# Gated linear attention and a bilinear FFN on one core: the values term of four chunks in 128x32 tiles, with tokens put in order when y is evicted

## The chip, the cores and the metric

The kernel runs on one core of a Trainium2 chip. The metric is device time in microseconds (us): three runs of the kernel before gave 193.74, 194.33 and 194.84, median 194.33.

## What is computed

```python
# q, k, v, alpha: [4, 8, 768, 48] float32 (batch, head, token, dim)
for t in range(S):
    state = alpha[:, :, t, :, None] * state + einsum('bhd,bhe->bhde', k[:, :, t], v[:, :, t])
    y[:, :, t] = einsum('bhd,bhde->bhe', q[:, :, t], state)
x = y.transpose(0, 2, 1, 3).reshape(3072, 384)
out = ((x @ w_a) * (x @ w_b)) @ w_out        # w_a, w_b [384, 1536], w_out [1536, 384]
```

Each head carries a 48x48 state that decays by alpha at every token. The outputs of the eight heads stand side by side as the 384 inputs of the FFN.

## The kernel before

**Chunks.** The work is cut into six chunks. Chunk c covers two batches (`ch.b0`) and 256 tokens (`ch.s`), so chunks 0 and 1 are the first third of the sequence, 2 and 3 the second, 4 and 5 the last. A chunk has two units u (one per batch); the 256 tokens of a unit lie on 128 partitions, two neighbouring tokens per partition: token 2p + r is on partition p with rank r (`load`, L549). Partitions 0 to 63 and 64 to 127 are the groups g = 0 and 1, of 128 tokens each. HC is 64, C is 128, D is 48, DP is 64.

**Steps of one chunk**, by the names that the order uses:
- `ld a/k/q/v`: loads. v is cast to bfloat16 by the DMA, so GpSimd issues it (POOL's queue); a, k and q come from POOL's or SyncE's (SP's) queue.
- `ln`, `ra`, `l2`, `l2s`, `R`, `AQ` (or `H`, `L`, `A2`), `E`, `lv`, `mq`, `mk`: logarithms and cumulative sums of alpha, their exponentials, and q and k scaled by them into QKp (L678). `dr`, `dl` write and read the decays through DRAM for bls.
- `C`/`Ce` (chunks 0 and 1: PE transposes, L736, and their copies, L744 and L742) or `T` (chunks 2 to 5: DMA transposes from SP's queue, L767) give kqT, queries and keys with the dims on the partitions.
- `v`: copies the loaded values into the padded tile vxs, heads 96 apart, zeros between (L785 on ScalarE, L787 on VectorE). Two vxs tiles alternate between chunks.
- `K`, `K2`, `k`: the states (L799, L812 on PE; L826 to L830 on VectorE).
- `D`: scores of queries against keys (L841), 16 matmuls in 64x64 tiles, each 128 columns (queries) wide; group g of the keys goes to PSUM partitions of half g, rank rk to a block of the columns.
- `M` (L846) or `Mc` with `Mm` (L850, L854): the scores leave PSUM times the causal mask, as bfloat16 m.
- `SB`, `SA` (`carried`): queries times the carried states, opening the sums of y in two PSUM banks; `Y` (`inner`, L865): values times m added to them. Y takes 48 matmuls: 12 pieces of 64 rows of y (the 384 rows of a unit's y don't fall on head borders, so a piece covers parts of one or two heads, and the padding zeros keep the other heads out), times two ranks, times two groups, in 64x64 tiles.
- `X` (`evac`, L900, L902): evicts y into xT. In xT and all that follows, the columns of a 128-token block stand by rank, then by partition, not in token order.
- `a`, `b` (`ff`, L919): the two FFN products of 128 rows of d_ff, 3 matmuls each, 512 columns for a whole chunk (`*`) or 256 for a unit. `as` (L925): a's copy on ScalarE. `pr` (`ff_prod`, L933): their product on VectorE, which puts the tokens in order by a strided write. `o`, `oc` (L941, L952), `ot`, `otc` (L956, L958), `st`, `stc` (L974, L977): the last FFN product, 6 matmuls per half, its eviction and store.

**The order.** Every instruction's place is written out in the string PROGRAM: `chunk: step; step; ...`, with the engine (V, S, P, Y for VectorE, ScalarE, GpSimd, SyncE) or PSUM bank as the last argument. Each engine works its own instructions off in that order and waits where its data or a buffer is missing. FFN work of a chunk stands between the attention steps of the next. Beside L919, L941 and the like, PE has no other work. PSUM has eight banks; D, AQ and y take two neighbouring ones each. The a, k, q and v tiles have two buffers, m has four, `as_` three, xT two.

Of the kernel before, what the change touches and what calls it, by code (L numbers as in the profile page):

```python
# [53 lines left out]
0: as 0 1; b 6 * 0; b 11 * 3; a 8 * 4; pr 6 *; pr 11 *
2: ld a * P
0: b 0 1 1; as 8 *; a 3 1 6
1: E 0 b; lv 0 k V
0: a 10 * 2; pr 0 1
1: mq 0 V; ld v 1 P
0: b 8 * 4  # L60
1: A2 1 7
0: as 10 *; b 10 * 2; pr 8 *
1: E 1 b
0: as 3 1; as 7 *; b 9 * 3; b 3 1 0; b 7 * 1; a 9 * 6
2: ld q * P
1: v 0 S; lv 1 q V; mk 0 V
0: pr 10 *
1: mq 1 V; C 0 1 4
0: as 9 *
1: C 0 0 2  # L70
0: o 0 0 5; pr 7 *
1: dk * 6
2: ld k * P
3: ld v * P
0: cz 1 v P; pr 9 *
1: Ce 0 0 S; E 1 i; de *; lv 1 k P; Ce 0 1 V; D 0 1 1; D 0 0 3
0: pr 3 1
1: Mc 0 0; K2 0 0 7 0
0: o 1 0 6
1: mk 1 V; M 0 1  # L80
0: o 3 0 4; o 1 1 -; ot 1 S; c3 P
3: ld a * P
0: cs 1 0 P; o 3 1 -
1: k 0 0 V; k 0 1 V; Mm 0 0 V; SB 0 1; C 1 0 3; C 1 1 7
0: ot 3 S; o 0 1 -
1: Ce 1 0 V
2: ln *
1: v 1 V; D 1 0 3; Ce 1 1 S; K2 1 1 6 0; Y 0; SA 0
0: ot 0 V
1: k 1 0 V; D 1 1 6  # L90
0: o 2 0 5
1: M 1 0
2: l2 0 V
1: X 0 S; a 3 0 1; Mc 1 1
2: l2s 0 P; l2s 1 P
1: a 2 0 3; a 4 0 4
2: R 0
1: k 1 1 V; as 4 0
2: ra 1
1: as 3 0; b 4 0 7  # L100
0: o 2 1 -
1: as 2 0
0: ot 2 S
1: pr 4 0
2: R 1; lv 1 q P
1: b 3 0 6; b 2 0 7; a 5 0 2; pr 3 0; b 5 0 3; as 5 0; b 1 0 5; a 1 0 1; pr 5 0; pr 2 0; a 7 0 2; as 1 0; pr 1 0
2: AQ 3
1: SB 1 6
2: lv 0 k P
1: a 10 0 5  # L110
2: lv 1 k V; ra 0; ld v * P
1: Mm 1 1 V
2: E 1 b
1: as 10 0; b 10 0 0; pr 10 0
2: mq 1 V; E 1 i
1: as 7 0; b 7 0 1
2: E 0 b; E 0 i
1: a 0 0 5
0: st 3 Y
2: dr  # L120
1: SA 1; Y 1
2: mk 1 V
1: pr 7 0; a 11 0 0; a 6 0 3; b 6 0 2; X 1 S; b 11 0 4; a 2 1 6; as 6 0; a 3 1 7; as 11 0; b 2 1 1; pr 6 0
2: lv 0 q V
1: b 4 1 0; as 2 1
2: T 1
1: pr 11 0
2: dl
0: st 0 Y
1: a 0 1 2; pr 2 1  # L130
2: mq 0 V
1: b 3 1 3; b 0 0 6; as 3 1; as 0 0; b 0 1 7; pr 3 1; a 8 0 1; a 9 0 5
0: st 1 Y
1: b 8 0 3; b 9 0 4; pr 0 0; as 0 1
2: mk 0 V
1: a 4 1 2
3: ln *
1: a 9 1 6; pr 0 1; as 8 0; b 9 1 1
3: ra 1
1: b 10 1 7; pr 8 0; a 10 1 3; as 4 1; as 9 0; as 9 1; a 6 1 6; b 6 1 2; b 11 1 5; pr 4 1; as 10 1; pr 9 0; a 11 1 4; pr 10 1; pr 9 1; as 6 1  # L140
2: v 1 S
1: a 8 1 3; b 8 1 1; a 7 1 6; pr 6 1
3: l2 0 V
1: as 11 1
2: T 0
1: as 8 1; a 5 1 4
3: ra 0
1: as 5 1; a 1 1 2
2: v 0 V
4: ld a * Y  # L150
1: pr 11 1; as 7 1; pr 8 1
2: K2 * * 0 7; D 1 1 3; D 1 0 5
1: as 1 1; b 5 1 2; o 2 0 1
2: k * 0 V
1: pr 5 1
3: v 0 S; v 1 S
1: b 1 1 2
2: Mc 1 0; M 1 1
3: l2s 0 P; l2s 1 P
1: b 7 1 0; o 2 1 -; pr 1 1; o 3 0 4  # L160
2: SB 0 5
1: pr 7 1
3: R 0
2: D 0 0 2
1: ot 2 V
2: Mm 1 0 V
1: o 3 1 -
2: Mc 0 0; SB 1 0; D 0 1 2
3: R 1
1: ot 3 S  # L170
2: SA 0
1: o 0 0 4
0: cs 0 0 P
2: Mc 0 1
4: ln *
3: ld q * Y; ld k * Y
2: k * 1 V
3: AQ 2
2: Y 1; SA 1; Mm 0 1 V; Mm 0 0 V; Y 0; X 0 S
3: E 0 b  # L180
4: l2 0 V
2: X 1 V
1: o 0 1 -
2: b 1 * 6; a 1 * 5
3: E 1 b
4: ld k * Y
3: E 1 i
1: ot 0 S
3: E 0 i
4: l2s 0 P  # L190
2: a 0 * 0; b 0 * 1; as 0 *; as 1 *
3: lv 0 k P; lv 0 q P
2: a 5 * 7
1: st 3 Y
2: a 7 * 4
4: l2s 1 P
2: a 2 * 5
3: lv 1 q V; mq 1 V; lv 1 k V
2: pr 1 *
3: dr  # L200
2: pr 0 *
3: mk 0 V
4: ld q * Y
0: st 2 Y
2: as 5 *; a 6 * 6; b 6 * 2; as 7 *
3: mq 0 V
2: b 9 * 4; b 7 * 0
1: st 2 Y
3: dl
4: R 0  # L210
2: b 5 * 7
1: o 1 0 3
2: a 9 * 1; pr 7 *; as 6 *
3: T 0
2: pr 6 *
4: ra 0
2: pr 5 *; a 11 * 6
3: mk 1 V
2: as 9 *; a 3 * 0
4: lv 0 k V; lv 0 q V; R 1  # L220
2: as 2 *
1: o 1 1 -
2: as 11 *; a 8 * 5; b 11 * 2; a 4 * 7; b 2 * 1
3: T 1
1: ot 1 V
2: pr 9 *; as 8 *; pr 11 *; pr 2 *; b 8 * 3; b 4 * 5; as 4 *
5: ld a * Y
3: K2 * * 4 6
2: pr 8 *; as 3 *; pr 4 *
3: k * 0 V; D 0 0 2; Mc 0 0  # L230
2: b 3 * 1
4: ra 1
2: pr 3 *; b 10 * 5; a 10 * 0
3: D 1 0 1; D 1 1 3
2: as 10 *
3: k * 1 V; Mc 1 1
2: o 0 0 7; o 2 0 0
3: M 1 0
5: ln *
2: pr 10 *  # L240
4: lv 1 q P
3: SB 1 3; D 0 1 1; Mc 0 1
4: lv 1 k P
5: ld q * Y
1: st 0 Y
3: SB 0 5
2: o 2 1 -
3: Mm 1 1 V; Mm 0 0 V; Mm 0 1 V
4: ld v * P
2: ot 2 S; o 0 1 -  # L250
4: AQ 0; E 0 b; E 0 i
3: SA 0; Y 0; SA 1
4: E 1 b
3: Y 1
5: l2s 1 V
4: mq 0 V; mk 0 V
3: X 0 S; X 1 S
2: o 3 0 2; o 3 1 -
4: T 0
3: a 5 * 3  # L260
4: E 1 i; v 0 S
3: a 9 * 0
2: ot 3 S
3: b 5 * 6; a 6 * 5; as 5 *
2: st 2 Y
3: as 9 *
5: ld k * P; l2s 0 P
3: as 6 *
5: ra 1
4: mq 1 V  # L270
2: ot 0 S
3: a 0 * 1
4: mk 1 V
3: a 1 * 2
4: D 0 0 3
5: l2 0 V
1: st 1 Y
4: dr
5: R 0
3: pr 5 *  # L280
4: v 1 S; M 0 0
3: b 1 * 7; as 1 *; a 3 * 5; b 9 * 6; pr 9 *; b 6 * 4; a 2 * 0; pr 6 *
4: T 1
5: lv 0 k P
3: b 0 * 6; as 0 *; as 2 *
4: dl
3: a 8 * 1
5: lv 1 q P
3: b 4 * 0; a 4 * 4; b 2 * 3; pr 1 *; pr 0 *; as 8 *; pr 2 *; as 4 *; pr 4 *; b 3 * 6; b 8 * 2
5: ld v * P; lv 1 k P  # L290
3: a 11 * 1
5: ra 0
3: as 3 *; pr 8 *; as 11 *; a 7 * 0
4: D 1 0 3; K * 0 5
5: lv 0 q P
3: pr 3 *; as 7 *
5: v 1 V
4: k * 0 V
5: R 1
4: D 1 1 6; D 0 1 1; Mc 1 0; Mc 1 1; M 0 1  # L300
2: o 1 0 0; o 1 1 -
3: a 10 * 7; b 11 * 3
4: SB 1 4
2: ot 1 S
3: as 10 *
4: Mm 1 0 V
3: pr 11 *
4: SB 0 1
# [96 lines left out]
def kernel(  # L405
# [11 lines left out]
    nc = tc.nc  # L417
# [681 lines left out]
```

## Time and profile before

| | before |
|---|---|
| runs, us | 193.74, 194.33, 194.84 (median 194.33) |
| profiled execution: span from first to last instruction, us | 192.0 |
| the median's distance to that span, us (what lies around it; the page lists no other time of its own for the execution) | 2.3 |
| PE busy, us | 186.8 |
| VectorE (DVE), ScalarE (ACT), GpSimd (POOL) busy, us | 133.1, 106.5, 56.9 |
| granted TensorE clock | 1.00 |
| DMA packets, MB | 62618, 29.40 |
| read from HBM, MB | 25.98 |

The page's rows of digits cut the span into 40 slices of 4.8 us; a 9 is 90% busy or more. PE rows say when a matmul was in flight; since matmuls overlap, the time that one adds is read from the distance between the starts of neighbours, or from a piece of the chain, not from its own duration. The chain of waits follows the work back from the last instruction, at each step to what released it. The list of waits gives for each engine what ended its idle time.

### The profile page before, as it was taken

What the parts mean: (1) busy time and instruction counts of PE and PEld (TensorE: products, weight loads), DVE (VectorE), ACT (ScalarE), POOL (GpSimd) and SP (SyncE); (2) the same over time, 40 slices, a digit from 0 to 9 for tenths busy, and PEclk for the clock granted to TensorE, in tenths of its full rate; (3) what the DMA queues carried; (4) which work ended last, traced back from release to release, by engine and by line L of the source; (5) the groups of instructions that cost most, each with busy time, mean ns of one, the idle gap of its engine ahead of it and who ended that gap; (6) DMA issues with size and microseconds to landing.
All of it is one profiled execution on the core that took longest, in us unless ns stands there. A gap on an engine that the chain in (4) does not pass through costs nothing.

```text
span 192.0 us, 6086 instructions
## 1 busy us (share of the span) xinstructions
PE 186.8 (97%) x2613; PEld 116.9 (61%) x2613; DVE 133.1 (69%) x223; ACT 106.5 (55%) x194; POOL 56.9 (30%) x75
## 2 busy tenths in 40 slices
PE   7999999999999999999999999999999999999992
PEld 3888875677778876645557444656465644545562
DVE  2387698994989888899897956887567446252510
ACT  4448885656779867753487756743572435314211
POOL 8999626752450500640074262000000000000000
PEclk9999999999999999999999999999999999999999
DMA  5999999999969999999999989017641200000422
GB/s 132 274 219 218 251 253 235 244 269 264 251 107 166 165 216 265 248 254 149 233 213 181 156 174 129 3 42 140 146 66 44 85 0 0 0 0 3 164 82 82
DMA packets 62618, 29.40 MB, mean 153 GB/s; under 512 B 53712, under 2 KB 60768, under 8 KB 62592
## 3 DMA queue, kind: packets, MB, share of 16 engines
q0 software_dynamic: 18432, 13.37, 39.6%
q1 hardware_dynamic: 44016, 15.55, 38.1%
q8 instruction: 20, 0.33, 0.7%
q10 hardware_dynamic: 144, 0.10, 0.2%
q14 instruction: 6, 0.05, 0.1%
HBM read 25.98 MB, written 4.74 MB: 160 GB/s over the span
## 4 chain that ended last, share of the span: by engine, by line
PE 91%; DMA 5%; SPq 1%; DVE 1%; issue 1%; ACT 0%; DVEq 0%
PE psum L919 47%; PE psum L941 24%; PE psum L865 7%; PE psum L841 3%; DMA kqT<-QKp 3%; DMA q_t<-in_q_dram 3%; PE psum L736 2%; PE psum L633 1%; PE psum L952 1%; SPq L549 1%; PE psum L799 1%; PE psum L812 1%; PE psum L700 1%; PE psum L591 1%; PE psum L592 1%
## 5 line engine op out<-in xcount | busy, mean ns | idle before, releaser
L919 PE MATMUL psum<-xT,wb_t 128*128 128x512 bf16 (+1 forms) x270 | 56.0, 337 | 0.0
L919 PE MATMUL psum<-xT,wa_t 128*128 128x512 bf16 (+1 forms) x270 | 56.0, 337 | 0.0
L941 PE MATMUL psum<-wo_t,prod 128*128 128x384 bf16 x276 | 49.4, 326 | 0.0
L919 PEld LDWEIGHTS <-wb_t 128*128 128x128 bf16 x270 | 25.9, 98 | 19.9 <-issue 0.5
L919 PEld LDWEIGHTS <-wa_t 128*128 128x128 bf16 x270 | 25.9, 98 | 19.7 <-issue 0.3
L941 PEld LDWEIGHTS <-prod 128*128 128x128 bf16 x276 | 25.9, 98 | 17.6
L956 ACT ACTIVATE ot<-psum 128x384 f32<-128x384 f32 (+1 forms) x16 | 7.7, 482 | 22.7 <-PE psum L941 21.6
L850 ACT ACTIVATE m<-psum 128x1024 bf16<-128x1024 f32 x14 | 14.1, 1023 | 4.6 <-PE psum L841 4.3
L613 POOL TENSOR_TENSOR l<-la 64x384 f32<-64x384 f32 x7 | 7.8, 1108 | 26.6 <-ACT la L556 19.0
L846 DVE TENSOR_TENSOR m<-psum,mask 128x1024 bf16<-128x1024 f32 x10 | 12.1, 1220 | 3.1 <-PE psum L841 3.1
L652 POOL TENSOR_TENSOR q_t<-q_t,ra 128x384 f32<-128x384 f32 x5 | 6.1, 1215 | 22.5 <-ACT ra L645 19.7
L556 ACT ACTIVATE la<-a_t 128x1536 f32<-128x1536 f32 (+2 forms) x9 | 9.5, 1055 | 2.3 <-DMA a_t<-in_alpha_dram 2.2
L678 DVE TENSOR_TENSOR QKp<-q_t,beta 128x768 bf16<-128x768 f32 x10 | 10.0, 995 | 1.0 <-ACT beta L667 1.0
L865 PE MATMUL psum<-m,vx 64*64 64x128 bf16 x576 | 10.5, 217 | 0.0
L900 ACT ACTIVATE xT<-psum 128x768 bf16<-128x768 f32 x9 | 7.2, 816 | 5.7 <-PE psum L865 5.5
L678 DVE TENSOR_TENSOR QKp<-k_t,invb 128x768 bf16<-128x768 f32 x10 | 9.7, 972 | 0.8 <-ACT invb L667 0.8
L854 DVE TENSOR_TENSOR m<-m,mask 128x1024 bf16<-128x1024 bf16 x14 | 9.3, 684 | 1.2 <-ACT m L850 1.2
L958 DVE COPY ot<-psum 128x384 f32<-128x384 f32 (+1 forms) x9 | 4.8, 532 | 7.6 <-PE psum L941 4.7
L865 PEld LDWEIGHTS <-vx 64*64 64x64 bf16 x576 | 9.0, 107 | 0.5 <-issue 0.3
L841 PE MATMUL psum<-kqT 64*64 64x128 bf16 x384 | 9.0, 219 | 0.4 <-DMA kqT<-QKp 0.3
L652 POOL TENSOR_TENSOR k_t<-k_t,a_t 128x384 f32<-128x384 f32 x6 | 7.4, 1228 | 6.1 <-issue 3.3
L549 POOL DMA_DIRECT2D v_t<-in_v_dram x8 | 8.5, 1058 | 0.1
(271 smaller groups left out, 287.9 us busy)
## 6 DMA issues: line engine op xcount, KB each, us to landing
out_dram<-ot SPq DMA_DIRECT2D x23, 192.0 KB, 3.8
q_t<-in_q_dram SPq DMA_DIRECT2D x3, 768.0 KB, 6.5
a_t<-in_alpha_dram POOLq DMA_DIRECT2D x2, 768.0 KB, 15.2
k_t<-in_k_dram POOLq DMA_DIRECT2D x2, 768.0 KB, 12.1
v_t<-in_v_dram POOLq DMA_DIRECT2D x4, 384.0 KB, 7.0
a_t<-in_alpha_dram SPq DMA_DIRECT2D x2, 768.0 KB
k_t<-in_k_dram SPq DMA_DIRECT2D x2, 768.0 KB
a_t<-in_alpha_dram POOLq DMA_DIRECT2D x3, 384.0 KB, 8.5
```

The lines of the kernel that those rows point to most:

```text
L549: eng.dma_start(out=t[:, us, hs].rearrange("p b h r d -> p (b h) (r d)"), in_=src[ch.b0 + us.start:ch.b0 + us.stop, hs, ch.s * 2 * C:(ch.s ...
L556: nc.scalar.activation(out=ch.la[:, us, hs].rearrange("p b h r d -> p (b h r d)"), in_=ch.a[:, us, hs].rearrange("p b h r d -> p (b h r d) ...
L613: eng.tensor_add(ch.l2[(1 - g) * HC:(2 - g) * HC, 1], x[:, :, 0, :], x[:, :, 1, :])
L652: eng.tensor_mul(x, x, by)
L678: eng.tensor_mul(QKp[ch.c % 2][:, u, j, :, hs, :D], src[:, u, hs].rearrange("p h r d -> p r h d"), f)
L841: nc.tensor.matmul(s2[g * HC:(g + 1) * HC, r, p, rk, :], lhsT=turned_part(ch, u, 1, rk, 2 * h + p, g, rs), rhs=queriesT(ch, u, 2 * h + p, ...
L846: nc.vector.tensor_mul(m.rearrange("p r a k s -> p (r a) (k s)"), ch.s2[u, h].rearrange("p r a k s -> p (r a) (k s)"), maskn(4))
L850: nc.scalar.activation(out=m.rearrange("p r a k s -> p (r a) (k s)"), in_=ch.s2[u, h].rearrange("p r a k s -> p (r a) (k s)"), func=AF.Copy)
L854: eng.tensor_mul(x, x, maskn(4))
L865: nc.tensor.matmul(y[c * DP:(c + 1) * DP, g, j // 2 * C:(j // 2 + 1) * C], lhsT=lhsT, rhs=rhs, start=(g, c) not in begun, stop=False, skip ...
L919: nc.tensor.matmul(p, lhsT=(wa_t, wb_t)[w][:, kk, f * 128:(f + 1) * 128], rhs=ch.xT[:, kk, us, :], start=(kk == 0), stop=(kk == KT - 1))
L941: nc.tensor.matmul(op, lhsT=ch.prod[:, f, at:at + C], rhs=wo_t[:, f, :], start=(f == 0), stop=(f == NFF - 1))
```

## The change

For chunks 2 to 5 (`NR = 2`), the values term is written in other tiles:
- Values come from DRAM a second time, by four new DMAs per chunk (`lw`), straight into a padded tile vps: one DMA for each group g and rank rk, 64 partitions and 16 runs of 48 values each. In vps the two ranks of a group lie on the two halves of the partitions, and heads are 64 apart. vps is a view of vxs' storage; its zeros are set once per tile (`cz i w`) after chunks 0 and 1 are through with it. `K` reads the loaded v tile itself, and `v` is gone for these chunks.
- `D` writes rank rk to PSUM half rk and group g to a block of the columns. The mask for this form is copied from the old one (`cm2`).
- `Y` (`inner_rows`) sums over 128 partitions (both ranks of a group) at once and gives 32 rows of y per matmul: 16 slices times two groups, 32 matmuls in 128x32 tiles, four neighbours in different column quarters. It needs y opened by `SB` or `SA` before.

For all chunks, `X` is split into two evictions per unit, one per group, and each writes the tokens in order (a step of two columns); xT is laid out by 128-token block. `pr` then writes straight.

The order is written anew from the first line to the last, with the same number of `a`, `b`, `o`, `D`, `K`, `C` and `T` steps. Two `Ce` and three `ot` move from ScalarE to VectorE, and one `otc` the other way.

```diff
+    VP = D + DP // 2
+    NR = 2
+    mask2 = cst.tile([C, 2, HC], BF16, name="mask2")
     vxs = [cst.tile([C, 2, 2, H, VS], BF16, name=f"vx{i}") for i in range(2)]
+    vps = [t.rearrange("p b r h e -> p (b r h e)")[:, :4 * H * VP].rearrange("p (g b h e) -> p g b h e", g=2, b=2, h=H) for t in vxs]
...
+    def load_rows(ch, g, rk, eng):
+        at = ch.s * 2 * C + g * C
+        eng.dma_start(out=vps[ch.c % 2][rk * HC:(rk + 1) * HC, g, :, :, :D].rearrange("p b h d -> p (b h) d"),
+                      in_=v[ch.b0:ch.b0 + 2, :, at:at + C, :].rearrange("b h (s r) d -> r s (b h) d", r=2)[rk])
...
+    def values(ch, gs, u, rk, hd):
+        return ch.v[gs, u, hd, rk, :] if ch.c >= NR else vxs[ch.c % 2][gs, u, rk, hd, :D]
...
     def scores(ch, u, h, tag):
...
+                        rk, g = (y, x) if ch.c >= NR else (x, y)
                         rs = slice(r * DP, (r + 1) * DP)
-                        nc.tensor.matmul(s2[g * HC:(g + 1) * HC, r, p, rk, :], lhsT=turned_part(ch, u, 1, rk, 2 * h + p, g, rs),
+                        half, part_ = (rk, g) if ch.c >= NR else (g, rk)
+                        nc.tensor.matmul(s2[half * HC:(half + 1) * HC, r, p, part_, :], lhsT=turned_part(ch, u, 1, rk, 2 * h + p, g, rs),
...
+    SLICES = [(h, 3 * (h // 2) + j) for h in range(H) for j in ((0, 1) if h % 2 == 0 else (1, 2))]
+    RANKS = [[x for x in SLICES if x[1] % 4 == c] for c in range(4)]
+
+    def inner_rows(ch, u):
+        y, begun = ch.y[u]
+        vp = vps[ch.c % 2].rearrange("p g b h e -> p g b (h e)")
+        W32 = DP // 2
+        for n in reversed(range(len(SLICES) // 4)):
+            for g in range(2):
+                for c in range(4):
+                    h, j = RANKS[c][n]
+                    at = h * VP + W32 * j - D * h
+                    assert (g, c // 2) in begun
+                    nc.tensor.matmul(y[c * W32:(c + 1) * W32, g, j // 4 * C:(j // 4 + 1) * C], lhsT=vp[:, g, u, at:at + W32],
+                                     rhs=ch.m[u, h // 4][:, h % 2, h // 2 % 2, g, :], start=False, stop=False, skip_group_check=True)
...
-            ch.xT = wk.tile([128, KT, B, C], BF16, name="xT")
...
+            ch.xT = wk.tile([128, B, KT, C], BF16, name="xT")
+        evict(ch.xT[:, 2 * u + g].rearrange("p a (s r) -> p a r s", r=2),
+              ch.y[u][0][:, g, :KT * C].rearrange("p (a r s) -> p a r s", a=KT, r=2), eng)
...
-            nc.tensor.matmul(p, lhsT=(wa_t, wb_t)[w][:, kk, f * 128:(f + 1) * 128], rhs=ch.xT[:, kk, us, :], start=(kk == 0), stop=(kk == KT - 1))
+            nc.tensor.matmul(p, lhsT=(wa_t, wb_t)[w][:, kk, f * 128:(f + 1) * 128], rhs=ch.xT[:, us, kk, :], start=(kk == 0), stop=(kk == KT - 1))
...
-        o_, a_, b_ = tokens(ch.prod[:, f, :], us), columns(a[:, :n], n), columns(b, n)
-        nc.vector.tensor_mul(o_, a_, b_)
+        nc.vector.tensor_mul(ch.prod[:, f, us.start * C:us.stop * C], a[:, :n], b)
```

Of the new order, the stretch with chunk 1's last scores and the first `lw`:

```
1: C 1 1 2; Ce 1 1 V; C 1 0 3; Mm 0 0 V; D 0 1 4; M 0 1; SB 0 6
0: cs 1 0 P
2: l2s 0 P; l2s 1 P
0: o 1 1 -; ot 1 V; ot 3 V; st 3 Y
1: Ce 1 0 V
0: o 0 0 2
1: v 1 S
0: o 0 1 -; ot 0 S; st 0 Y
2: l2 0 V
1: K2 1 1 0 1; k 1 0 V; D 1 1 4; Y 0
2: R 0; R 1; ra 1; lv 1 q P
1: D 1 0 2; M 1 0; Mc 1 1; SA 0; X 0 1 S
0: o 2 0 0; o 2 1 -; ot 2 V
1: X 0 0 S; a 3 0 4; b 3 0 5; SB 1 6; as 3 0; pr 3 0
2: lv 0 k P
0: st 1 Y
2: ld v * P; AQ 2; E 1 i; E 1 b
1: b 10 0 0; a 2 0 4; k 1 1 V; b 6 0 5
2: E 0 b; E 0 i
1: a 10 0 1; as 10 0; Mm 1 1 V
0: cz 0 w P
2: dr; mq 1 V
1: a 4 0 3; as 4 0; pr 10 0; Y 1
2: lv 1 k V; mk 1 V; T 1
0: cm2 P
1: SA 1; as 2 0; b 2 0 1; b 4 0 0; pr 4 0
2: dl
1: b 0 0 4; a 1 0 2; X 1 1 S; X 1 0 V; a 11 0 3; a 0 0 7; as 1 0; b 1 0 0; pr 1 0
2: lw 0 0 P
1: pr 2 0; as 0 0; pr 0 0
2: lw 0 1 P
...
2: lw 1 0 P; lw 1 1 P
1: as 5 0; pr 5 0; b 3 1 2
0: cz 1 w P
```

and, shortened, where the DMA transposes and the other `lw` stand:

```
3: lw 0 0 P
...
2: mk 0 V
3: lw 0 1 P
...
3: lw 1 1 P
...
2: T 0
1: b 11 1 6; b 2 1 7
4: ld a * Y
3: ld q * Y
...
3: dl; lv 0 q P; mq 0 V; mk 1 V; T 0
...
4: ld v * P
...
4: lw 0 0 P; AQ 0; E 0 b
3: SB 0 2; SB 1 6
4: E 0 i; lw 0 1 P; lw 1 0 P
...
4: mk 0 V
2: ot 3 S
4: T 0
3: SA 1; SA 0; Mm 0 0 V; Y 0
...
5: lw 1 0 P; lw 1 1 P; dr
...
3: a 7 * 2
5: T 0
```

More of the change, by code (lines that the diff above doesn't have):

```diff
@@ new lines @@
+1: l2 1 V; H 1 V; L 1 V
+2: ld a * P
+0: as 1 1; b 1 1 3; pr 1 1; a 6 * 1
+1: A2 0 4; ra 0; lv 0 q V
+0: b 6 * 5
+1: dk * 6
+0: as 6 *
+1: ld v 1 P
+0: a 3 1 1; as 3 1; b 4 1 3; a 10 * 7
+1: de *
+0: pr 3 1; pr 6 *
+1: A2 1 1; E 0 b; mq 0 V
+2: ld q * P
+1: E 0 i; lv 0 k V; mk 0 V; E 1 b
+0: a 4 1 2; as 4 1; a 9 * 6
+2: ld k * P
+0: as 10 *; b 9 * 4; a 8 * 2
+3: ld v * P
+1: v 0 S
+0: a 11 * 5
+1: ra 1
+0: cz 1 v P; pr 4 1
+1: lv 1 q V; mq 1 V
+0: as 9 *; b 10 * 7; pr 10 *; b 8 * 3
+1: lv 1 k P
@@ L173 @@
+1: o 0 1 -
 0: cs 0 0 P
[L174 removed]
+3: E 1 b; lv 1 q V; E 0 b; dr; mq 1 V
+2: b 2 * 2; b 7 * 3; a 7 * 6
 4: ln *
[L176 to L186, printed above, removed]
[L187 to L200 removed]
@@ L506, in const_mask, with const_mask2 @@
                                 pattern=[[-1, HC]], channel_multiplier=1)
+    def const_mask2(eng):
+        for rk in range(2):
+            ks = slice(rk * HC, (rk + 1) * HC)
+            ENG[eng].tensor_copy(mask2[ks], mask[ks, rk])
     def const_zero(i, what, eng):
```

570 lines of the change are left out of this document (226 added, 344 removed).

## The prediction

> **What bounds the kernel now.** I read the page's first lines, then PE's waits, then the chain of waits in order of time, then the groups by shape, and last the DMA queues by window. The page:
>
> ```profile
> span 192.0 us, 6086 instructions
> ...
> PE 186.8 (97%) x2613; PEld 116.9 (61%) x2613; DVE 133.1 (69%) x223; ACT 106.5 (55%) x194; POOL 56.9 (30%) x75
> ...
> PEclk9999999999999999999999999999999999999999
> DMA  5999999999969999999999989017641200000422
> ...
> PE 91%; DMA 5%; SPq 1%; DVE 1%; issue 1%; ACT 0%; DVEq 0%
> ```
>
> PE holds the chain at the full clock. DMA is the second full row, up to about 115 us. A busy PE alone proves little, so next the list of all that PE waited for:
>
> ```profile
> PE psum L574 <- DVE og L472: 1.2, 1, 1.2
> PE psum L841 <- DMA kqT<-QKp: 0.3, 1, 0.3
> PE psum L736 <- DVE QKp L678: 0.2, 1, 0.2
> ```
>
> After the opening PE waited 0.5 us in all. So the time is the sum of what PE streams, from 8.9 to 188.7 us in the chain. Only a shorter stream gains; any new wait costs in full. The tightest place is the 0.3: the scores D (L841) of chunk 4 waiting for a transpose. The 5% of DMA in the chain is otherwise no wait: it is this transpose's time, during which PE did FFN work.
>
> **The values term (Y).** The groups that price it (line, tile rows*columns, operands, count | busy us, mean ns):
>
> ```profile
> L865 PE MATMUL psum<-m,vx 64*64 64x128 bf16 x576 | 10.5, 217 | 0.0
> ...
> L736 PE MATMUL psum<-ident,QKp 128*128 128x128 bf16 x64 | 4.6, 220 | 0.2 <-DVE QKp L678 0.2
> ...
> L700 PE MATMUL psum<-og,la 128*48 128x2 f32 x64 | 1.8, 186 | 0.0
> ```
>
> and the chain in order of time (start, us, what; x counts instructions):
>
> ```profile
> 14.90 0.84 PE psum L700 x32
> ...
> 45.00 1.00 PE psum L736 x16
> ...
> 68.92 0.97 PE psum L941 x6
> 69.89 0.66 PE psum L919 x6
> ...
> 73.01 1.08 PE psum L941 x6
> 74.09 0.29 PE psum L865 x12
> ...
> 74.61 0.17 PE psum L865 x12
> ...
> 129.08 1.80 PE psum L865 x120
> ```
>
> A matmul lasts 217 ns, but they overlap: the chain passes 120 of the 64x64 ones (two Y, two SA) in 1.80 us, 15.0 ns each, 60 ns for four at a time. One Y is 48 of them, 0.72 us. The new Y is 2 g x 16 slices = 32 matmuls of 128x32 with the same 128 columns. The trace has no 128x32 tile. From below: four at a time and free weight loads, as now. From above: one at a time, as the full-width transposes (L736, 1.00/16 = 62 ns), 32 x 62 = 2.0 us, 1.3 more than now. The shortest stretch of twelve, 0.17 us, gives 14.2 ns as the lower end. I take 15.0: the new one too is four tiles over 128 columns, and L736 shows that a load for all 128 rows hides under the matmul before it. Saved: 16 x 15.0 ns = 0.24 us per Y, eight Y (chunks 2 to 5): **-1.92 us**.
>
> The Trainium skill speaks against this (page "TensorE: Matmul & The Clock Gate", Part 3, The mechanism): a weight load overlaps running matmuls only when its row group differs, and four 128x32 tiles share all rows. L736 shows the overlap with all rows shared, so I leave the sum as it is and keep the rule's case as rival 3.
>
> **Changes of tile shape.** Six o matmuls (L941) take 0.97 us when 128x128 work follows and 1.08 when 64x64 work does: 0.1 us per border. Y now differs from SA too. Marking the borders along both written orders gives 55 before and 60 after: **+0.5 us** (0, if 64x64 to 128x32 is free, to 0.5).
>
> **The a, b, o, D, SA, SB, K and C work** has the same counts and widths in both orders; scores only swap loops, and K reads the loaded values instead of their copy. The reordered xT is read in runs of 128 columns; no row shows its cost, I take 0 (a half-width a or b runs at 110 ns against 216, so the width costs nothing extra).
>
> **ACT and DVE.** Gone: five value copies on ACT (L785, 850 ns) and three on DVE (L787, 350 ns). Y's eviction (L900, L902) becomes halves: from 9 x 816 ns on ACT and 3 x 952 on DVE to 15 and 9 halves, which I price by ot's 128x384 rows, 482 and 554 ns: ACT as now, DVE +2.1. The token order moves from prod's write (L933, about 730 ns per 512; DVE's 192- and 384-wide rows, 359 and 552 ns, extend to 681) to the eviction: 0 to -2.6 us over 54 full products. Three ot and two kqT evictions go to DVE (+3.0; ACT -3.5). Net ACT about -7 us, DVE +1 to +4: hidden under PE, worth nothing on the path. Where this cover is thin: from chunk 1's mk 1 to chunk 2's AQ the new order gives DVE one mk (0.97), three Ce (2.1), one Mm (0.7), two M (2.4), two ot (1.1), three state steps (1.4), l2 (0.55) and R 0, R 1 (2.05), 11.3 us of rows within 11.9 us of PE work. AQ takes the two PSUM banks that the last M must free. Before, DVE was busy for 9.48 of the 10 us from 30 to 40 and PE waited for nothing.
>
> **GpSimd and the DMAs.** Sixteen lw are added. On POOL each issues like a v load (L549, 1.06 us): 17 us on an engine busy 57, plus under 2 us of memsets and mask copies. Each lw is 1024 runs of 48 values. A v load (2048 runs) shows the rate of packets, and what a transpose does beside one.
>
> ```profile
> q0 software_dynamic: 1840, 0.35, 169.0%
> ```
>
> This is the DMA view of 57 to 59.5 us (packets, MB, share): 1840 packets in 2.5 us. The same view of 113 to 116 us, and then of 116 to 120 us:
>
> ```profile
> q1 hardware_dynamic: 1806, 0.48, 106.5%
> ...
> v_t<-in_v_dram POOLq DMA_DIRECT2D x1, 384.0 KB, 8.1
> ...
> kqT<-QKp SPq DMA_TRANSPOSE x1
> ```
>
> ```profile
> q0 software_dynamic: 2064, 0.39, 118.1%
> ```
>  By packets an lw is 1024/736 = 1.4 us, by bytes half; I take 1.4, near POOL's own pace, 5.6 us per chunk, 22 in all. From 113 to 116 us only the transpose's queue (q1) moved, though the v load had been issued at 112.04; its packets (q0) come in 116 to 120. So a transpose holds a GpSimd load back. The other direction, a transpose issued behind such loads, the trace doesn't show: between no delay and the whole rest of the loads.
>
> When are they due? Adding PE's rows along the written orders (a or b 0.65 or 0.33, o 0.98, D 0.23, K2 of two 0.55, and so on) gives this PE work between a transpose's place and the first D that reads it, against 4.3 to 5.9 us from issue to landing: T 0 of chunks 2, 3, 4, 5 before 6.0, 6.8, 4.0, 4.1; after 5.9, 7.7, 6.5, 9.2. The lw of chunks 2 and 3 (POOL about 54 to 64 us) are due at Y at 77 and 105; those of chunk 4 start after v at about 98, those of 5 at 118, due at 128 and 148. T 1 of chunk 2 falls into chunk 2's lw with 12.4 us to spare, T 0 of chunk 4 (104.5) right behind chunk 4's. SP's loads a 4, q 3, k 3 stand behind T 0 of chunk 2: k 3, which GpSimd waited for until 79.8 us, comes 2 us later, and T 0 of chunk 3 has 7.7 - 5.1 = 2.6 us for it. Behind cz 1 w, which must wait for chunk 1's Y 1, POOL has only lw and l2s that nobody needs before 72 us. I take 0.3 us for all of it, what the one tight transpose cost before.
>
> **Sum**: -1.92 + 0.5 + 0.3 = -1.1 us. The end (last oc, ACT eviction, store) keeps its length. Against the profiled span of 192.0 this gives 190.9; the median of the runs, 194.33, is 2.3 above the span, which I leave as it is: **193.2 us**.
>
> **Rivals.**
> 1. The gain is eaten by one wait of about a microsecond: AQ of chunk 2, if DVE's 11.3 us don't fit, or a D half a transpose late. For it: two full resources and slacks of about a microsecond (5.9 and 6.5 against 5.1). Against: DVE rows overlap by nearly 0.1 us each in the timeline. 194.33 - 1.4 + 1.3 = 194.2.
> 2. Slower: transposes stand behind GpSimd's loads. T 1 of chunk 2 then waits out lw of chunks 2 and 3, packets to 66 us, and lands near 70.5 for a D at 67.5: 3 us. T 0 of chunk 4 waits for v and four lw: up to 2 us over its 6.5. 194.33 - 1.4 + 5 = 197.9. It decides from a delay of 7 us in chunk 2 or 1.4 us in chunk 4. Against: the one meeting in the trace went the other way. The skill's page "DMA: Bandwidth & Descriptors" (Queues, rings and completion order) says that an engine takes turns between queue rows packet by packet, which would double a transpose to about 10 us: enough room in chunk 2, about a microsecond late in chunk 4. The row above doesn't show such turns.
> 3. The tiles don't do what they are for: each weight load shows. L700 is the nearest row with narrow tiles of 128 rows: 32 pairs of load and matmul in 0.84 us, 26 ns each. 32 x 26 ns = 0.83 us on top of 0.48, against 0.72: +0.59 per Y, +4.7, +0.5: 199.5.
>
> **Chances.** Forecast 0.45 (its own range 192.2, at 14.2 ns without border costs, to 193.4); rival 1 0.24; rival 2 0.23; rival 3 0.08. Half a percent, 0.97 us, is about what a measurement of this kernel can tell from no change (the three runs lie within 0.3% of their median): faster 0.45, same 0.24, slower 0.31. The range reaches over rival 2: 192.2 to 198.0; rival 3 and the rest are left out.
>
> **What would show it.** A Y of chunk 2 to 5 passes in about 0.48 us (32 matmuls); 0.9 or more says rival 3. PE's list of waits stays under 1 us after the opening; D (L841) waiting for kqT by microseconds, with q0 packets running from the transpose's issue on, is rival 2; AQ behind M is rival 1. Transposes should still land in 4 to 6 us. The forecast is wrong if PE idles anywhere for over a microsecond, for then the 1.4 us are gone.

## The result and the profile after

The changed kernel took 213.43 us (median of four runs, 211.83 to 214.77) against 194.06 us for the kernel before on the same chip: a ratio of 1.0993, with a 95% interval of 1.0929 to 1.1057. Slower by 19.4 us, where 1.1 us faster was forecast, and outside the range.

The page of the profiled execution (its time 20.2 us over the span of before), with the rows that were shown of before:

```profile
span 212.2 us, 5857 instructions
...
PE 189.1 (89%) x2484; PEld 116.5 (55%) x2485; DVE 139.1 (66%) x230; ACT 99.4 (47%) x191; POOL 71.4 (34%) x95
...
PEclk9999999999999999999999755999999999999998
DMA  6999999999999999989999990992591110010024
```

PE was busy for 2.3 us more only; the rest is idle time. The clock row has a dip in three slices (5.3 us each here), 117 to 133 us by their place. What PE waited for:

```profile
PE psum L790 <- DMA kqT<-QKp: 16.7, 4, 12.7
PE psum L518 <- DVE og L402: 1.2, 1, 1.2
PE psum L878 <- DVE prod L891: 0.8, 2, 0.6
```

The 0.3 us of before has become 16.7, in four waits: scores D (L790 now) for a transpose, of chunk 2 (0.60 and 1.55 us) and of chunk 4 (12.68 and 1.92). The chain of waits in order of time shows the long one from its cause:

```profile
107.70 20.96 DMA kqT<-QKp
...
129.77 3.82 PE psum L878 x11
133.59 9.77 DMA kqT<-QKp
...
150.03 1.01 PE psum L847 x64
```

Chunk 4's first transpose took 21 us from issue to landing; before, such transposes took 4.3 to 5.9. The last line is the new values term and it does what was hoped: 64 matmuls (two Y) in 1.01 us, 15.8 ns each.

What moved meanwhile? The DMA view of 113 to 118 us (packets, MB, share of the 16 engines):

```profile
q0 software_dynamic: 57, 0.22, 75.9%
q1 hardware_dynamic: 324, 0.08, 55.8%
```

No packet of a row load (`lw`; "rows" from here on) is left by then: chunk 4's ended at 113.1. q0 is the load of chunk 5's k, in packets of 4 KB, and q1 the transpose. Both are "busy", and together they move 0.30 MB in 5 us; at the 250 GB/s of the page's full slices it would be 1.25 MB. In the packet records of this window half of the k packets still take 0.23 us or less, but a quarter take over 2.1, the longest 4.6; of the transpose's 256-byte packets half take 27 ns or less, a quarter over 230, the longest 466. I call this the crawl. VectorE and GpSimd aren't in it: from 119 to 128 us neither did any work, and it went on. The order of issue just before it, in the timeline:

```profile
107.53 1.23 POOL L488 DMA_DIRECT2D k_t<-in_k_dram  x1
...
107.70 1.34 SPq L711 DMA_TRANSPOSE kqT<-QKp  x1
```

In the kernel before the k load was issued 5.9 us ahead of the transpose:

```profile
100.57 1.17 POOL L549 DMA_DIRECT2D k_t<-in_k_dram  x1
...
106.47 3.03 SPq L767 DMA_TRANSPOSE kqT<-QKp  x1
```

Its packets were through at 107.3, a third of a microsecond ahead of the transpose's first.

The wait has a tail. The windows (us, PE busy, granted clock, DMA share, GB/s):

```profile
116.00:122.00 6.00, 0.03 (x1) 0.75 1.12 74
122.00:129.00 7.00, 0.30 (x12) 0.50 0.83 90
129.00:135.00 6.00, 6.00 (x50) 0.70 0.66 56
```

The clock figures are means over each window; cut finer, the clock is 0.50 from 118.95 to 132.60 us and 1.00 on both sides. So after 13 idle microseconds PE worked on at half the clock, from 129 to 135 at 0.70 in the mean: an estimated 6 x 0.30 = 1.8 us more. The sum: the waits after the opening are 18.5 us (16.75 for kqT, 1.7 for masks and products), against 0.5 before; with the 1.8 that is 19.8 of the 20.2.

### The profile page after: what moved, and what is told of

The parts are those of the page before. It is cut to its first block, busy times and chain, and to the rows that moved or that the text cites. A ratio compares the mean times of both kernels' runs of the same rounds, so it can differ in the third digit from the quotient of the medians.

```text
span 212.2 us, 5857 instructions
## 1 busy us (share of the span) xinstructions
PE 189.1 (89%) x2484; PEld 116.5 (55%) x2485; DVE 139.1 (66%) x230; ACT 99.4 (47%) x191; POOL 71.4 (34%) x95
## 2 busy tenths in 40 slices
DMA packets 79258, 30.96 MB, mean 146 GB/s; under 512 B 70352, under 2 KB 77408, under 8 KB 79232
## 4 chain that ended last, share of the span: by engine, by line
PE 35%; DMA 14%; DVE 1%; ACT 0%; issue 0%
PE psum L878 19%; DMA kqT<-QKp 14%; PE psum L899 11%; PE psum L790 1%; PE psum L816 1%; PE psum L847 1%; PE psum L910 1%; DVE m L797 1%; PE psum L746 0%; ACT ot L914 0%
## 5 line engine op out<-in xcount | busy, mean ns | idle before, releaser
L878 PE MATMUL psum<-xT,wb_t 128*128 128x512 bf16 (+1 forms) x270 | 57.4, 339 | 0.7 <-DVE prod L891 0.6
L878 PE MATMUL psum<-xT,wa_t 128*128 128x512 bf16 (+1 forms) x270 | 57.5, 340 | 0.2 <-DVE prod L891 0.2
L790 PE MATMUL psum<-kqT 64*64 64x128 bf16 x384 | 9.4, 227 | 16.9 <-DMA kqT<-QKp 16.7
L916 DVE COPY ot<-psum 128x384 f32<-128x384 f32 x11 | 6.0, 552 | 19.1 <-DMA out_dram<-ot 13.1
L790 PEld LDWEIGHTS <-kqT 64*64 64x64 bf16 x384 | 6.5, 111 | 19.8 <-DMA kqT<-QKp 17.9
L914 ACT ACTIVATE ot<-psum 128x384 f32<-128x384 f32 (+1 forms) x14 | 6.4, 467 | 16.7 <-PE psum L899 16.0
L596 POOL TENSOR_TENSOR k_t<-k_t,a_t 128x384 f32<-128x384 f32 x6 | 6.7, 1124 | 21.7 <-issue 18.7
L493 POOL DMA_DIRECT2D vx<-in_v_dram x16 | 13.1, 842 | 0.3 <-POOL vx L448 0.3
L914 ACT ACTIVATE xT<-psum 128x384 bf16<-128x384 f32 x15 | 8.3, 600 | 7.5 <-PE psum L847 4.4
L805 DVE TENSOR_TENSOR m<-m,mask 128x1024 bf16<-128x1024 bf16 x14 | 10.3, 745 | 0.8 <-ACT m L801 0.6
L622 DVE TENSOR_TENSOR QKp<-k_t,invb 128x768 bf16<-128x768 f32 x10 | 10.3, 1029 | 0.5 <-POOL k_t L596 0.3
```

The source lines that it names most:

```text
L493: eng.dma_start(out=vps[ch.c % 2][rk * HC:(rk + 1) * HC, g, :, :, :D].rearrange("p b h d -> p (b h) d"), in_=v[ch.b0:ch.b0 + 2, :, at:at + ...
L596: eng.tensor_mul(x, x, by)
L622: eng.tensor_mul(QKp[ch.c % 2][:, u, j, :, hs, :D], src[:, u, hs].rearrange("p h r d -> p r h d"), f)
L790: nc.tensor.matmul(s2[half * HC:(half + 1) * HC, r, p, part_, :], lhsT=turned_part(ch, u, 1, rk, 2 * h + p, g, rs), rhs=queriesT(ch, u, 2 ...
L805: eng.tensor_mul(x, x, maskn(ch, 4))
L878: nc.tensor.matmul(p, lhsT=(wa_t, wb_t)[w][:, kk, f * 128:(f + 1) * 128], rhs=ch.xT[:, us, kk, :], start=(kk == 0), stop=(kk == KT - 1))
```

## The experiments

My first theory, A: the time goes where GpSimd's loads and the transposes' packets lie beside each other. Its first rival, B: the 16,640 added packets (16,384 of 96 bytes, the rest of 4) cost wherever they lie.

### First round: take the rows, the k load, or both away from the transposes

**e1_no_rows**: `lw` does nothing and vps is filled with zeros whole, so the values term of chunks 2 to 5 is left out of the result.

```diff
-        "lw": lambda x, g, r, e: load_rows(x, int(g), int(r), ENG[e]),
+        "lw": lambda x, g, r, e: None,
```

> The changed kernel with its sixteen lw DMAs left out; the padded value tiles hold zeros instead, so the values term of chunks 2 to 5 is missing from y. All else, k of chunk 5 on GpSimd's queue too, stays. Theory A (a DMA transpose and a GpSimd load in flight together slow one another down, above all T 0 of chunk 4 beside the load of k for chunk 5): the small waits on the transposes of chunk 2 and on T 1 of chunk 4 (4.1 us together) go, but v and k of chunk 5 are still issued within a few us of T 0 of chunk 4, so the 12.7 us wait stays or shrinks only by part: 198 to 209 us. Rival B (the sixteen additional transfers are the cost, by their number of packets): 192.5 to 194 us, PE waiting under 1 us for kqT.

Measured: 197.22 us (in brackets, here and below: the ratio to the kernel before on the same chip, and its 95% interval: 1.0165, 1.0137 to 1.0194). Below A's span, above B's: no wait for kqT is left, and without lw in front of it the k load went out at 101.73, 3.4 us ahead of the transpose. So the rows do 16 of the 19 us, in one of two ways: as packets, or by pushing the k load back. 3 us have nothing to do with rows.

**e2_k5_behind**: the k load moves to SP's queue, behind the transpose.

```diff
 4: T 0
+5: ld k * Y
...
-5: ld k * P
```

> The changed kernel with one DMA moved: k of chunk 5 goes from GpSimd's queue to SP's, directly behind T 0 of chunk 4; all sixteen lw stay where they are. Theory A: the 12.7 us wait and the slow clock after it go, the waits beside lw (0.6, 1.6 and 1.9 us) stay: 195 to 199 us. Rival B: the packets are as many as before, 209 to 214 us.

Measured: 206.87 us (1.0674, 1.0629 to 1.0719), between the two. The 12.7 us wait is gone: chunk 4's first transpose lay beside rows alone (the k load's packets came after it) and landed 7.7 us after its issue. But the edit made waits of its own: stores on SP now stand behind the k load, VectorE waited 4.16 us for a free ot buffer, PE 2.9 us for VectorE, and 2.4 us for chunk 4's second transpose, which lay beside chunk 5's rows. After both waits the clock dropped to 0.50 (121.95 to 125.37 and 135.61 to 139.02 us).

**e3_old_k5_late**: the kernel before, its k load one step later in GpSimd's order.

```diff
-5: ld k * P; l2s 0 P
+5: l2s 0 P; ld k * P
```

> The kernel before with two neighbours swapped on GpSimd: k of chunk 5 is issued behind l2s 0 of chunk 5, some 4 us later, so that its packets run together with T 0 of chunk 4. No lw, no 128x32 tile, not a packet more. Theory A: T 0 of chunk 4 takes 10 us or more to land instead of 5.0, PE waits 5 to 13 us for it, 200 to 209 us. Rival B: within a microsecond of the kernel before, 193.5 to 195 us.

Measured: two runs, 196.08 and 199.79 us (the trace is the longer one's). Issued 1.8 us ahead of the transpose, the k load kept its pace (half of its packets took 0.21 us or less, nine in ten 0.47 or less); the transpose's last packet came 7.6 us after its issue and PE waited 3.4. A loss without any row, but no crawl: this fits neither number well.

**e4_all_clear**: e2's edit, and all row loads of chunks 2, 3 and 4 behind gates, a tiny GpSimd copy that reads the landed transpose.

```diff
 3: ld k * Y; l2s 1 P
+2: gatet 0; lw 0 0 P; lw 0 1 P; lw 1 0 P; lw 1 1 P
+0: cz 1 w P
+3: lw 0 0 P; lw 0 1 P; lw 1 0 P; lw 1 1 P
...
-4: D 0 1 4; M 0 1; D 0 0 6; M 0 0; mq 1 V; T 1; dl
+4: D 0 1 4; M 0 1; D 0 0 6; M 0 0; mq 1 V; T 1; dl; gatet 1; lw 0 0 P; lw 0 1 P; lw 1 0 P; lw 1 1 P
```

> The changed kernel with GpSimd's loads kept out of the transposes' time: k of chunk 5 as in e2, and the lw of chunks 2 and 3 issued only after T 0 of chunk 2 has landed, those of chunk 4 only after its T 1 (a one-element copy of kqT on GpSimd waits for it). The same sixteen lw and the same tiles. Theory A: every transpose lands in 4 to 6 us, PE waits for kqT under 1 us, and the shorter Y shows: 192.5 to 194.5 us. Rival B: over 205 us. A third case: the lw come too late for Y of chunk 2, which then waits 1 to 4 us: 195 to 198 us.

Measured: 211.72 us (1.0922, 1.0894 to 1.0949). A's number failed, but by a new wait, not the old one. In PE's waits no kqT is left, and there is:

```profile
PE psum L842 <- DMA vx<-in_v_dram: 7.9, 2, 5.1
```

Rows behind chunk 2's last transpose (69 us) can't be there for chunk 2's Y at 77. A further 4.39 us PE waited for a mask from VectorE, which had itself waited 7.14 us for GpSimd, busy issuing rows. The experiment showed that places must be found, not that places don't matter.

### Second round: all rows kept, each in a clear slot; and the k load beside a transpose alone

**e5_clear_slots**: chunk 2's rows stay; chunk 3's go behind chunk 2's last transpose, chunk 4's behind its own first, chunk 5's (and its values load) behind chunk 4's second; the k load goes ahead of chunk 4's values load.

```diff
 0: cs 0 0 P
+2: gatet 0
+3: lw 0 0 P; lw 0 1 P; lw 1 0 P; lw 1 1 P
...
 4: R 1; ra 1; lv 1 q P
+5: ld k * P
...
 5: l2s 0 P
+4: gatet 0; lw 0 0 P; lw 0 1 P; lw 1 0 P; lw 1 1 P
...
 5: lv 1 k P; lv 0 q P
+4: gatet 1
+5: ld v * P; lw 0 0 P; lw 0 1 P; lw 1 0 P; lw 1 1 P
```

> All the row loads stay, in other places: chunk 2's where they were, chunk 3's behind chunk 2's last transpose has landed, chunk 4's behind its first transpose has landed, chunk 5's (with its values load) behind chunk 4's second transpose has landed; the load of chunk 5's k goes ahead of chunk 4's values load. Theory A (the time is lost where GpSimd's loads and the transposes' packets lie beside each other, and nowhere else): no wait on kqT over 1 us from 76 us on, at most 2.2 us of such waits in chunk 2; 197 to 201 us, that is the kernel without row loads (197.2) and chunk 2's remainder. Theory B (16,640 more packets of 96 bytes cost wherever they lie, by transfers that come late): the waits move to other loads or to vx, 203 us or more.

Measured: 196.5 us (1.0114, 1.0072 to 1.0155), a little under A's span. From its page, and the head of PE's waits:

```profile
PE 186.2 (95%) x2484; PEld 115.3 (59%) x2485; DVE 138.7 (71%) x230; ACT 99.3 (51%) x191; POOL 72.7 (37%) x98
...
DMA packets 79258, 30.96 MB, mean 158 GB/s; under 512 B 70352, under 2 KB 77408, under 8 KB 79232
```

```profile
PE psum L876 <- DVE prod L889: 2.5, 3, 1.3
```

The same 79258 packets as in the changed kernel, and 16.9 us less. B is out: place is what counts. The transposes land after 5.5 to 6.8 us and none is waited for.

**e6_old_k5_beside**: the kernel before, with `l2s` and two memsets (`pad`, 1.35 us each) put ahead of its k load, which so goes out 1.0 us behind the issue of the transpose.

```diff
-5: ld k * P; l2s 0 P
+5: l2s 0 P; pad P; pad P; ld k * P
```

> The kernel before, without any row loads: two memsets of 1.5 us on GpSimd hold the load of chunk 5's k back to about 107.6 us, 1 us behind the issue of chunk 4's first transpose. Theory A (a transpose and one GpSimd load of 4 KB packets that lie wholly beside each other crawl by themselves): the transpose takes 15 to 21 us instead of 4.5, PE waits 10 us or more for it, 205 to 212 us. Rival C (it took the row loads as a third party; two alone are dealt with in turns): the transpose lands within 9 us, 195 to 200 us.

Measured: 194.86 us (1.0038, 1.0018 to 1.0058). A as it stood is wrong here. The k load's packets came only when the transpose's were done (107.4 to 110.9, then 110.9 to 114.5); the transpose's last packet came 4.7 us after its issue. So a third party seemed needed, the rows: theory G of the next round.

**e7_k5_act**: the changed kernel, its k load issued by ScalarE.

```diff
+5: ld k * S
 4: T 0
...
-5: ld k * P
```

> The changed kernel, with the load of chunk 5's k issued by ScalarE at about 106.8 us instead of by GpSimd at 107.5 us; everything else stays, the row loads of chunk 4 at 104.3 to 107.6 us too. Theory A (the crawl needs GpSimd's own descriptors and queue): chunk 4's first transpose lands within 10 us, PE waits at most 3 us for it, 198 to 207 us. Rival F (any load of such size beside a transpose): it lands after 15 us or more, 209 to 214 us.

Measured: 207.08 us (1.067, 1.0618 to 1.0722). ScalarE got to the issue at 108.40, not 106.8, 0.7 us behind the transpose. Its load runs in a queue of its own (q10) in packets of 384 bytes, from 111.7 to 120.6 us, and so beside the transpose's (110.7 to 118.6), nearly one for one: 755 and 752 packets from 114 to 118 us. The transpose took 11.6 us to land, and PE waited 8.7 us for kqT in four waits, 3.5 the longest, for that one. This is between the two theories: over A's 10 us, far under F's 15. The edit changed the packets' size along with the issuing engine, so it doesn't show which of the two keeps the crawl away. What rows alone do to chunk 4's first transpose, e2 showed: 7.7 us, not 21.

**e8_clear_ot_act**: e5, three evictions of ot on ScalarE instead of VectorE.

```diff
-1: ot 1 V
-2: o 0 1 -; ot 0 V
+1: ot 1 S
+2: o 0 1 -; ot 0 S
...
-2: ot 1 V
+2: ot 1 S
```

> As the kernel with clear slots, and three evictions of ot behind chunk 3's values term go from VectorE to ScalarE (1.8 us of VectorE's work at 0.54 to 0.60 us each). Theory D (the part of the loss that stays without row loads, some 3 us, is VectorE: it worked without a gap from 100 to 119 us there, and PE waited 1.4 us for an eviction of ot and 0.8 us for masks and products behind it): 1.5 to 3 us faster than the kernel with clear slots, no wait for ot. Rival E (the remainder is PE's own borders and not VectorE): within 0.5 us of the kernel with clear slots.

Measured: 197.02 us (1.0151, 1.0115 to 1.0187), 0.5 us above e5: D, in this form, fell. The wait at 120 us changed its name (1.0 us for ScalarE), and another came to 2.75 us: the load of chunk 3's k, behind chunk 3's rows, held GpSimd for 2.45 us, VectorE behind it, and PE for a product.

### Third round: what makes the crawl

**e9_pads_for_lw4**: the changed kernel, two pads in place of chunk 4's four lw, so that the k load keeps its time (chunk 4's values term reads chunk 2's rows).

> The changed kernel without the four row loads of chunk 4 (its values term then reads chunk 2's rows): two memsets of 1.5 us keep GpSimd as long, so that the load of chunk 5's k is still issued at about 107.3 us, beside the first transpose of chunk 4 at 107.7 us. Theory G (the crawl needs three parties: row packets ahead of the k load in GpSimd's queue let both it and the transpose begin in the middle of each other; two alone are served one after the other): the transpose lands within 8 us, 198 to 203 us. Rival H (the k load and the transpose crawl in any case when they are issued together): it lands after 15 us or more, 208 to 214 us.

Measured: 198.43 us (1.022, 1.0195 to 1.0246). The k load went out 0.64 us ahead of the transpose; its packets were first (108.2 to 112.0), the transpose's mostly after them (109.9 to 115.2), the last 8.3 us after issue. G seemed right.

**e10_old_k5_together**: e6 with one pad instead of two.

```diff
-5: ld k * P; l2s 0 P
+5: l2s 0 P; pad P; ld k * P
```

> The kernel before, no row loads: one memset of 1.5 us on GpSimd puts the issue of chunk 5's k at about 106.1 us, within 0.3 us of the first transpose of chunk 4 (106.3), between the two cases already seen (104.7: transpose done 7.6 us after its issue; 107.25: 4.7 us). Theory G: within 9 us, 194 to 199 us. Rival H: 15 us or more, 204 to 212 us.

Measured: 210.21 us (1.0794, 1.0737 to 1.0851). Theory G falls: the kernel before, with no row and nothing changed but `l2s` and a memset ahead of a load, which so goes out 5.5 us later, loses 16 us. (With a second memset, e6, it loses 0.8.) Its timeline and PE's waits:

```profile
106.12 1.19 POOL L550 DMA_DIRECT2D k_t<-in_k_dram  x1
...
106.52 1.32 SPq L768 DMA_TRANSPOSE kqT<-QKp  x1
```

```profile
PE psum L842 <- DMA kqT<-QKp: 14.6, 1, 14.6
```

and for comparison e6, whose transpose was not disturbed:

```profile
106.24 1.32 SPq L768 DMA_TRANSPOSE kqT<-QKp  x1
...
107.25 1.19 POOL L550 DMA_DIRECT2D k_t<-in_k_dram  x1
```

One thing adds to e10's size: chunk 4's second transpose was issued at 112.13 us, into the crawl. It didn't start it: from 110 to 112 us only 139 of the first transpose's packets came through, where 770 had come in the two microseconds before.

All cases with the k load on GpSimd, by its issue relative to that of the transpose (us), the transpose's time from issue to its last packet (for e10 and after: to its landing by the chain), and whose packets began first:

| kernel | k load's issue minus transpose's | transpose took | packets |
|---|---|---|---|
| before | -5.9 | 4.5 | k through before |
| e1, e12 | -3.4 | 6.2, 6.6 | k first, then transpose |
| e3 | -1.8 | 7.6 | k first |
| e9 | -0.64 | 8.3 | k first |
| e10 | -0.40 | 19.3 | transpose first, k 0.9 us later, in between |
| after | -0.17 | 21.0 | transpose first, k 1.4 us later, in between |
| e6 | +1.0 | 4.7 | transpose, then k |

Theory H: the crawl needs no rows. It comes when the k load's packets begin in the middle of the transpose's; here that was with issues 0.2 and 0.4 us apart. Wider apart, one of the two goes first.

**e14_k5_gated** puts H on the changed kernel: one gate, rows untouched.

```diff
+4: gatet 0
 5: ld k * P
```

> The changed kernel with one edit: GpSimd issues the load of chunk 5's k only when chunk 4's first transpose has landed; the row loads stay where they are. Theory H (the crawl comes of a k load and a transpose that are issued within half a microsecond of each other): the transpose meets row packets alone, as in the run with ScalarE's load, and lands in 7 to 11 us; PE waits 1 to 4 us there; 201 to 207 us. Rival (the row packets are enough for the crawl): above 209 us.

Measured: 200.26 us (1.0329, 1.0293 to 1.0365), a little under H's span: 13.2 us back by one line. The transpose lay beside the rows and landed after some 7.5 us; no wait of PE's for kqT is left. PE waited 2.9 us elsewhere, for VectorE, which stood 4.35 us behind GpSimd's late l2s. The clock then fell (0.50 from 119.86 to 123.27 us, 0.61 as the mean of this window):

```profile
119.00:123.00 4.00, 3.50 (x10) 0.61 0.13 32
```

**e12_lw4_later**: the changed kernel, only chunk 4's rows moved behind its first transpose.

```diff
-4: lw 0 0 P; AQ 0; E 0 b
+4: AQ 0; E 0 b
...
-4: E 0 i; lw 0 1 P; lw 1 0 P
+4: E 0 i
...
-4: lv 0 q V; mq 0 V; lw 1 1 P
+4: lv 0 q V; mq 0 V
...
 5: l2s 0 P
+4: gatet 0; lw 0 0 P; lw 0 1 P; lw 1 0 P; lw 1 1 P
```

> The changed kernel with one edit: the four row loads of chunk 4 wait until that chunk's first transpose has landed, so that the load of chunk 5's k follows the values load directly, at about 104.3 us. Theory A (place is what counts, and this one place most of all): the wait of 12.7 us and the low clock after it are gone, chunk 2's 2.2 us stay, and chunk 5's rows may cost 1 to 3 us beside chunk 4's second transpose; 198 to 203 us. Rival B (the rows' volume): the waits move on, above 206 us.

Measured: 197.47, 197.58, 204.35 and 204.42 us, median 200.96; the ratio of the first two is 1.0176 (1.0144 to 1.0209), and the trace is of the last. So either the time is just under A's span or just over it, and B's is not reached. In the trace the wait of 12.7 us is gone; the second transpose of chunk 4 lay beside chunk 5's values and row loads, PE waited 3.7 us for it and went on at a clock of 0.50 from 133.1 to 136.5. Why two runs lost some 7 us and two didn't stays open.

### The last two microseconds

**e11_clear_k3_early**: e5, chunk 3's k load right behind chunk 2's first transpose, two evictions of ot on ScalarE.

```diff
 2: dl
+3: ld k * Y
...
-3: ld k * Y; l2s 1 P
+3: l2s 1 P
...
-1: ot 1 V
-2: o 0 1 -; ot 0 V
+1: ot 1 S
+2: o 0 1 -; ot 0 S
```

> The kernel with clear slots, and two edits for what is left there: the load of chunk 3's k is issued on SP right behind chunk 2's first transpose, not after its second one and two more loads (GpSimd waited 0.8 us for it at 83 us, and PE 1.1 us for the product queued behind that on VectorE), and two evictions of ot at 110 us go to ScalarE (PE waited 1.3 us at 120 us for a product). Theory D (what is left over the kernel before, 2.4 us, is these two waits): both under 0.5 us, 194 to 195.2 us. Rival E (it is in PE's own stream): still 196 to 197 us.

Measured: 197.88 us (1.0214, 1.0165 to 1.0263), over both spans. The wait at 88 us fell from 1.1 to 0.5, that at 120 stayed at 1.3: two masks and chunk 4's product (1.76 us) stand ahead of the FFN product there, the evictions weren't it.

**e13_clear_prod_first**: e5, the k load as in e11, and the FFN product ahead of chunk 4's product.

```diff
-4: D 0 1 4; M 0 1; D 0 0 6; M 0 0; mq 1 V; T 1; dl
-3: b 9 * 0; a 0 * 1; a 9 * 2; as 9 *; b 6 * 4; pr 6 *; a 3 * 5
+4: D 0 1 4; M 0 1; D 0 0 6; M 0 0
+3: b 9 * 0; a 0 * 1; a 9 * 2; as 9 *; b 6 * 4; pr 6 *
+4: mq 1 V; T 1; dl
+3: a 3 * 5
```

> The kernel with clear slots, with the load of chunk 3's k issued on SP right behind chunk 2's first transpose, and with chunk 4's last product for its second transpose (1.84 us on VectorE at 118 us, beside GpSimd's work) put behind the FFN product that PE waited 1.3 us for. Theory D (what is left are such waits for VectorE): the two waits together fall from 2.4 us to under 0.8 us, 194.3 to 195.5 us. Rival E (it is in PE's own stream, or a new wait takes their place): 196 us or more.

Measured: 196.13 us (1.0118, 1.0088 to 1.0148). The wait at 120 us is gone, and yet the time is E's. The head of PE's waits:

```profile
PE psum L879 <- DVE prod L892: 1.3, 3, 0.6
...
PE psum L791 <- DMA kqT<-QKp: 0.7, 1, 0.7
```

Both were partly right. By the distances from each matmul's start to the next, PE's stretch is 2.35 us longer than before: 2.2 us of waits (2.61 against 0.44) and 0.2 of stream. In the stream, values times m fell from 8.82 to 7.33 us; queries times states rose from 4.70 to 5.77, a and b from 94.82 to 95.17, the rest by 0.3 in all.

Part of that 0.2 belongs to the waits. The list counts a wait from the end of the last matmul, so that matmul's run-out is booked as stream: ahead of the 0.62 us wait at 84.5 us it is 1.00 us from start to start, where such matmuls start 0.22 apart, so 0.16 more were lost. Over e13's six waits this comes to 1.2 us, over the two of before to 0.3. By this estimate the stream without waits is some 0.7 us shorter than before. No version here beats the kernel before.

## Why the prediction was wrong, step by step

- **Y, -1.92 us**: right in kind, a little high. 15.8 ns per matmul instead of 15.0: 1.01 us for two Y instead of 1.44, -1.7 over eight (e13's distances give 1.5). Rival 3 (weight loads show) is out.
- **Borders, +0.5**: counted right (55 and 60 in the traces), priced a little low. Where queries times states ends at another tile shape, the next matmul starts 0.15 us on instead of 0.015; e13 has 13 such places, before had 8: about +0.7 us. The stream's forecast of -1.4 was not reached in any case: e13 measured +0.2, or some -0.7 by the estimate above, without what its waits add.
- **The step that failed: "I take 0.3 us for all of it"**, for GpSimd's and the DMAs' side. It measured some 18.5 us: 16.75 of waits for transposes and about 1.8 of low clock behind them. Two things went wrong in it. First, the list of what is due when had chunk 4's v and four lw ahead of T 0, and left out what the four lw push back: the k load of chunk 5, the next DMA on the same engine. 3.27 us of issue carried it from 104.34, 3.4 us ahead of the transpose (e12, where only these four stand elsewhere), to 107.53, 0.17 us ahead. e1, e9 and e14 each undo this and give back 13 to 16 us. Second, its price: "between no delay and the whole rest of the loads" bounds a transpose that waits its turn, not one that takes 21 us because both sides slow down; the row loads ended at 113.1 us, the transpose landed at 128.7.
- **"A transpose holds a GpSimd load back"** was read from one meeting and was right for that one, as in e6. With another order of issue (e3, e9) the load goes first, and with issues close together (after, e10) neither does.
- **Rival 2** had the direction and, for chunk 2, the size: 3 us forecast, 0.60 + 1.55 measured. For chunk 4 it forecast 2 and it was 12.7. It was given 0.23. The doubling to about 10 us by turns, which it also weighs and which the one meeting before hadn't shown, is what rows do: 438 packets of theirs and 438 of the transpose's passed in 71 to 72 us, and the two transposes that lay in them, chunk 2's last and chunk 4's second, took 10.4 and 9.8 us. The 21 us are another thing.
- **The clock** was in no term. It cost about 1.8 us in the changed kernel and has a part in most of the slower experiments.
- **lw, 1.4 us each**: right. Chunk 4's 4096 packets ran from 107.8 to 113.1. POOL grew by 14.5 us (17 forecast), ACT by -7.1 (-7 forecast), DVE by 6.0 (1 to 4 forecast). Rival 1's AQ of chunk 2 waited 0.3 us.
- **k 3, "2 us later", with room**: about right. GpSimd waited 0.33 us for it, and 0.8 to 2.5 where chunk 3's rows lay in its way (e5, e8).

What is shown: rows in other places cost no more than no rows at all (e5, 1.0114, against e1, 1.0165); the k load close to the transpose costs 13 us with rows (after against e14) and 16 without (e10, where the second transpose came on top). What stays open: why the two slow each other so far. The trace gives long packets, not what they wait for; VectorE isn't it, with no work from 113 to 125 us in e10 and from 119 to 128 in the changed kernel. How near two issues must be is known by the table's cases only: the limits lie between 0.40 and 0.64 us ahead, and between 0.17 us ahead and 1.0 us behind. Other sizes of load weren't tried.

## What to carry to other kernels

When a change adds DMA issues to an engine's queue, list every later DMA of that queue with its new time of issue, and look for transposes issued within a microsecond: the load that is pushed can cost far more than the loads that push it. A DMA transpose on the critical path wants its own clear stretch. One gate on GpSimd gave it one here (e14), at the price of what then stood behind the gate (4.35 us of VectorE's). Price a wait of 2.4 us or more with the clock behind it, and check a saving in the stream against the tile borders that it adds.

## What the runs showed of the hardware that was not expected

- A transpose and one GpSimd load of 768 KB whose packets begin within each other took 19 to 21 us instead of 4.5 (e10, after). With the load issued 1.0 us behind, its first packet came 3.6 us after issue, where 1.9 and 2.6 were seen with the v load out of the way (e3, e10), and the transpose lost nothing (e6, 4.7 us).
- Beside packets of about its own size the transpose took turns, one for one: 438 and 438 with rows of 96 bytes (after, 71 to 72 us), 755 and 752 with ScalarE's load of 384-byte packets (e7, 114 to 118 us). It then took 10.4 and 11.6 us.
- Between the opening and the end the granted clock was 1.00 or 0.50. It fell to 0.50 after or in waits of 2.41 us and more: for 3.41 us after 2.41 (e2), 2.88 (e14) and 3.70 (e12), for 6.83 with 3.42 (e3), for 13.65 with 12.68 (after). After 1.36 us (e1) it stayed at 1.00, and once after 2.75 us too (e8). The Trainium skill (page "TensorE: Matmul & The Clock Gate", section "What's actually happening") puts the fall at an idle window of some 3.4 us, to half the clock. The half agrees, and the stretches are one, two and four times 3.41 us; the waits of 2.41 and 2.88 us are shorter than that window, and no run here shows why they were enough.
- VectorE's product into QKp takes 0.95 us, and 1.74 to 1.84 while GpSimd works on products of its own (e5: 84.7 and 117.9 us).
